# A matmul-bound kernel: the first normalized half cut in two, and the last masks counted longer by the builder

## The chip, the cores and the metric

One core of one Trainium2 chip. The metric is the device time of one execution in microseconds, lower is better; a figure quoted for a kernel is the median of its runs.

The engines go by short names: PE is the matmul engine and PEld its weight loads, DVE the vector engine, ACT the scalar engine, POOL GpSimd. A load "lands" when its data has arrived. Times inside a profile are microseconds from the start of its span.

## The reference

The whole is `x + A(xn) + B(xn)` with `xn = layernorm(x)`, for x of 2048 x 1024 in bf16.

```python
h = _layernorm(x)                               # B is given xn: a second layernorm
u = gelu(einsum('bsd,sf->bdf', h, w1) + b1)     # mixes over the 2048 tokens; F = 3584
y = einsum('bdf,fs->bds', u, w2) + b2
# A: 32 heads of 32, four segments of 512 tokens; in each segment
p = softmax(q k^T * scale + mask)               # causal
o = g * (phi(q) M) / (phi(q) z) + (1 - g) * (p v)
M, z = M + phi(k)^T v, z + sum(phi(k))
# and then o @ wo
```

## The kernel before

Every instruction goes out through a builder that keeps its own clock: each operation has an estimated `ns`, and PE's work in the attention part is ordered by when the builder believes operands ready. A wrong estimate makes no wrong result, only another order. PE is to be kept full with "fill": the matmuls of the second MLP product and of the output projection, in two streams, taken whenever no attention matmul is believed ready.

The start. PE is kept busy with warm-ups, matmuls of zeros, until the first data is there. x comes in 16 row chunks of 128; h is its normalized form, and the chunks are the contraction of the first MLP product, so PE can begin with chunk 0 as soon as its h is there. Eight banks collect four column blocks of w1 by two halves of h.

```python
def warm(self):                                  # N_WARM = 14
    with fw.group(reads=[R[0]], writes=[self.R_bank[7]], ns=self.N_WARM * 300):
        for _ in range(self.N_WARM):
            fw.mm(self.bank(7), z[:, 0:P], z, start=True, stop=True)

def norm_and_first_hidden(self):
    self.stats(0); self.scale(0); self.stats(1)
    self.ln_h(0, 0)          # DVE: half of h, 512 columns
    self.ln_h(0, 1)
    self.scale(1); self.ln_h(1, 0); self.ln_h(1, 1)
    self.early_hidden(0)     # PE: 8 matmuls of 512 columns
    # ... statistics of the later chunks: even ones and chunk 1 on ACT, others on DVE
    self.stats(3, 0); self.stats(3, 1, False)
    self.scale(2); self.ln_h(2, 0); self.ln_h(2, 1)
    self.aggregate(3)
    self.early_hidden(1)
    # ... then chunk after chunk
```

The attention part. The logits come in 46 steps of at most seven banks. ACT takes each bank through the exponential into a slot of pT, POOL masks it there, and "weighings" multiply the slots by v. The results of four heads (a unit) are then combined on DVE, transposed by a transfer and multiplied by wo: the last 72 matmuls of the program are such projections. A step is laid out so:

```python
fl.op({"act": (... exp ..., 575, 488)}, [], [R[slot]], box=box[i], give=True)
ns = 225 + 115 * len(masks)
fl.op({"pool": (... affine_select ..., ns, ns + 30)}, [R[slot]], [R[slot]])
```

The softmax here doesn't subtract the row's maximum and nothing guards it: scores larger than these inputs give would overflow.

## Time and profile before

| | kernel before |
|---|---|
| time, first three runs | 690.88 us (690.82 to 691.54) |
| span of the profile | 689.3 us |
| PE busy | 685.0 us, 99% |
| DVE, ACT, POOL busy | 34%, 45%, 22% |
| first matmul of chunk 0 / first weight load of chunk 3 | 6.64 / 12.44 us |
| last step's logits / last 72 projections start | 666.07 / 672.90 us |

The page's first part says who is full; here only PE. The chain of waits then says which of the few idle times of PE matter: it goes back from the last instruction to whatever released each step. Everything that lies ahead of 12.44 us on that chain is ACT, DVE, POOL and a landing. The lines are in the prediction.

### The profile page before, as it was taken

The numbers are of one execution on the slowest core, as the hardware profiler recorded it, in microseconds if no ns is written. First come the engines' busy times: TensorE is split into PE (matmuls) and PEld (weight loads), VectorE is DVE, ScalarE is ACT, GpSimd is POOL, SyncE is SP. The second block draws the span as 40 slices with busy tenths as digits, with TensorE's granted clock in tenths as the row PEclk, the third lists the DMA queues.
The fourth block names the chain that finished last, engine by engine and source line by source line (L and its number), as shares of the span: only waits on it lengthen the run. The fifth ranks groups of instructions, "written<-read, shape, count | busy, mean of one in ns | idle before, by whom it ended". The sixth has DMA issues, their size and how long they took to land.

```text
span 689.3 us, 12154 instructions
## 1 busy us (share of the span) xinstructions
PE 685.0 (99%) x4855; PEld 327.3 (47%) x4855; DVE 234.8 (34%) x505; ACT 309.6 (45%) x611; POOL 153.9 (22%) x379
## 2 busy tenths in 40 slices
PE   9999999999999999999999999999999999999998
PEld 3444444444444454444454444544544444544554
DVE  6631100000001242434462461743636333451524
ACT  7331111111134475755645472745756453544540
POOL 4820000000001232323312131313333131312330
DMA  9367666325027657657547566474564546445334
GB/s 310 119 178 182 160 156 202 100 61 144 1 93 169 147 133 151 143 121 183 131 95 166 123 134 143 100 170 99 131 145 108 124 115 156 106 104 139 79 86 137
DMA packets 275714, 92.06 MB, mean 134 GB/s; under 512 B 234186, under 2 KB 272074, under 8 KB 275658
## 3 DMA queue, kind: packets, MB, share of 16 engines
q1 hardware_dynamic: 275658, 91.28, 53.5%
q8 instruction: 39, 0.64, 0.4%
q14 instruction: 17, 0.14, 0.1%
HBM read 74.47 MB, written 5.24 MB: 116 GB/s over the span
## 4 chain that ended last, share of the span: by engine, by line
PE 97%; ACT 1%; DMA 1%; POOL 0%; DVE 0%; SPq 0%; issue 0%; POOLq 0%; DVEq 0%
PE ps_all L217 97%; DMA xin<-in_A_x_dram 1%; ACT xn_tmp L850 0%; POOL pT L1158 0%; DVE h L891 0%; SPq L247 0%; ACT xn_tmp L852 0%; ACT pT L1150 0%; POOL ln_r L883 0%; POOLq L581 0%; DVE fin L1356 0%; POOL ln_t L881 0%; DVE ln_mv L866 0%; DVEq L65 0%
## 5 line engine op out<-in xcount | busy, mean ns | idle before, releaser
L1158 POOL TENSOR_SCALAR_AFFINE_SELECT pT<-pT 128x256 bf16<-128x256 bf16 (+1 forms) x320 | 127.6, 408 | 504.2 <-ACT pT L1150 494.7
L1150 ACT ACTIVATE pT<-ps_all 128x512 bf16<-128x512 f32 x320 | 161.9, 618 | 76.8 <-PE ps_all L217 76.8
L217 PE MATMUL ps_all<-h,w1all 128*128 128x512 bf16 x896 | 193.9, 379 | 0.3 <-DVE h L891 0.2
L217 PEld LDWEIGHTS ps_all<-h,w1all 128*128 128x128 bf16 x896 | 87.5, 98 | 106.5 <-issue 0.9
L217 PE MATMUL ps_all<-gT,w2n 128*128 128x512 bf16 x560 | 124.1, 379 | 0.0
L1005 ACT ACTIVATE gT<-ps_all,bc 128x512 bf16<-128x512 f32 x56 | 37.8, 690 | 140.6 <-PE ps_all L217 140.6
L217 PE MATMUL ps_all<-gT,w2l 128*128 128x512 bf16 x325 | 86.0, 380 | 0.0
L217 PEld LDWEIGHTS ps_all<-gT,w2n 128*128 128x128 bf16 x560 | 54.4, 98 | 64.0 <-DMA w2n<-in_B_w_dram 0.2
L1220 ACT ACTIVATE ost<-ps_all 128x264 bf16<-128x264 f32 (+1 forms) x97 | 34.0, 379 | 75.3 <-PE ps_all L217 74.0
L1479 DVE SCALAR_TENSOR_TENSOR stg<-ps_all,bc,stg 128x512 bf16<-128x512 f32 x32 | 23.9, 746 | 124.9 <-PE ps_all L217 124.9
L217 PE MATMUL ps_all<-xnT,wk 128*128 128x512 bf16 x256 | 60.5, 379 | 0.0
L217 PE MATMUL ps_all<-xnT,wq 128*128 128x512 bf16 x256 | 60.4, 379 | 0.0
L217 PE MATMUL ps_all<-wv_sb,xnT 128*128 128x512 bf16 x256 | 60.2, 379 | 0.0
L217 PEld LDWEIGHTS ps_all<-vA,pT 128*128 128x128 bf16 x1280 | 41.2, 96 | 5.5 <-POOL pT L1158 1.0
L217 PEld LDWEIGHTS ps_all<-gT,w2l 128*128 128x128 bf16 x325 | 27.6, 97 | 33.7 <-issue 10.1
L217 PE MATMUL ps_all<-vA,pT 128*128 128x33 bf16 x1280 | 42.8, 177 | 0.3 <-POOL pT L1158 0.3
L943 DVE TENSOR_SCALAR gcol<-gcol 128x32 f32<-128x32 f32 x1 | 0.2, 182 | 118.6 <-ACT gcol L941 118.6
L217 PEld LDWEIGHTS ps_all<-xnT,wk 128*128 128x128 bf16 x256 | 25.1, 98 | 30.2
L217 PEld LDWEIGHTS ps_all<-wv_sb,xnT 128*128 128x128 bf16 x256 | 24.9, 98 | 30.5 <-ACT pT L1150 4.0
L1031 ACT ACTIVATE kT<-ps_all 128x512 bf16<-128x512 f32 x32 | 19.1, 597 | 43.2 <-PE ps_all L217 43.2
L217 PEld LDWEIGHTS ps_all<-xnT,wq 128*128 128x128 bf16 x256 | 23.4, 97 | 29.5 <-issue 6.4
L217 PE MATMUL ps_all<-wo_sb,oT 128*128 128x512 bf16 x128 | 31.2, 379 | 0.0
(74 smaller groups left out, 482.9 us busy)
## 6 DMA issues: line engine op xcount, KB each, us to landing
w2n<-in_B_w_dram SPq DMA_DIRECT2D x100, 160.0 KB, 2.7
w1all<-in_B_w_dram SPq DMA_DIRECT2D x12, 1024.0 KB, 5.2
w2l<-in_B_w_dram SPq DMA_DIRECT2D x73, 128.0 KB, 2.4
wq<-in_A_wq_dram SPq DMA_DIRECT2D x32, 256.0 KB, 2.9
wk<-in_A_wk_dram SPq DMA_DIRECT2D x32, 256.0 KB, 3.2
stg<-in_A_x_dram SPq DMA_DIRECT2D x32, 128.0 KB, 2.6
out_dram<-stg SPq DMA_DIRECT2D x32, 128.0 KB, 2.1
xin<-in_A_x_dram SPq DMA_DIRECT2D x5, 512.0 KB, 6.5
```

Source lines behind the costliest of these rows:

```text
L217: ins = self.nc.tensor.matmul(out, *args, **kwargs)
L943: fw.op("dve", lambda e: e.tensor_scalar(self.gcol[:], self.gcol[:], 1.0, None, op0=ALU.add), reads=[self.R_gcol], writes=[self.R_gcol])
L1005: fw.op("act", lambda e: e.activation(self.gT[:, fc, half * 512:(half + 1) * 512], self.bank(b), ACT.Gelu_apprx_tanh, bias=self.b1c[:, fc: ...
L1031: self.flow.op({"act": (lambda e, b: e.activation(dst, view(self.bank(b)), ACT.Copy), 585, 540), "dve": (lambda e, b: e.tensor_copy(dst, v ...
L1150: fl.op({"act": (lambda e, b, slot=slot: e.activation(pT[:, slot, :], self.bank(b), ACT.Exp, scale=SCALE), 575, 488)}, [], [R[slot]], box= ...
L1158: fl.op({"pool": (lambda e, ap=ap, pat=pat: e.affine_select(ap, ap, pattern=pat, compare_op=ALU.is_ge, fill=0.0, base=0, channel_multiplie ...
L1220: "act": (lambda e, b: e.activation(dst, self.ps[:, b, 0:n * VW], ACT.Copy), 175 + n * 27, 140 + n * 27)},
L1479: engs={"dve": (lambda e, b: e.scalar_tensor_tensor(dst, k.bank(b), k.b2c[:, c:c + 1], dst, op0=ALU.add, op1=ALU.add), 750, 785)},
```

## The change

Two things. The first quarter of h of chunk 0 is made apart, so that PE may begin on it sooner. Its bank then has two matmuls for its two column halves, and a start flag on both would not do (the prediction says why), so the last four warm-up matmuls write zeros with the start flag into banks 0, 2, 4 and 6, and the eight quarter matmuls only accumulate. Second, the builder counts the masks of the last two steps 200 ns longer.

```diff
 def warm(self):
-    with fw.group(..., writes=[self.R_bank[7]], ...):
-        for _ in range(self.N_WARM):
-            fw.mm(self.bank(7), z[:, 0:P], z, start=True, stop=True)
+    with fw.group(..., writes=[self.R_bank[b] for b in (0, 2, 4, 6, 7)], ...):
+        for i in range(self.N_WARM):
+            b = 2 * (i - self.N_WARM + 4) if i >= self.N_WARM - 4 else 7
+            fw.mm(self.bank(b), z[:, 0:P], z, start=True, stop=(b == 7))
 # norm_and_first_hidden
-    self.ln_h(0, 0)
+    self.ln_h(0, 0, True)     # two operations of 256 columns, the second waits for the first
 # early_hidden
+    if c == 0:
+        for q in range(2):
+            for fc in range(self.N_EARLY):
+                with fw.group(reads=[self.R_w1f[0], self.R_h[0][0] if q else self.R_h0], ...):
+                    fw.mm(self.ps[:, 2 * fc, 256 * q:256 * q + 256], ...,
+                          self.h[:, 0, 256 * q:256 * q + 256], start=False, stop=False)
 # step
-    ns = 225 + 115 * len(masks)
+    ns = (225 if n < self.n_steps - 2 else 425) + 115 * len(masks)
```

More of the change, by code (lines that the diff above doesn't have):

```diff
@@ L676, in alloc @@
         self.R_xnt = [Res(f"xnt{i}") for i in range(4)]
+        self.R_h0 = Res("h0q")
         self.R_h = [[Res(f"h{c}_{hf}") for hf in range(2)] for c in range(N_TCH)]
@@ L801, in warm @@
         fw.op("dve", lambda e: e.memset(z, 0.0), writes=[R[0]])
-        with fw.group(reads=[R[0]], writes=[self.R_bank[7]], ns=self.N_WARM * 300):
-            for _ in range(self.N_WARM):
-                fw.mm(self.bank(7), z[:, 0:P], z, start=True, stop=True)
+        with fw.group(reads=[R[0]], writes=[self.R_bank[b] for b in (0, 2, 4, 6, 7)], ns=self.N_WARM * 300):
+            for i in range(self.N_WARM):
+                b = 2 * (i - self.N_WARM + 4) if i >= self.N_WARM - 4 else 7
+                fw.mm(self.bank(b), z[:, 0:P], z, start=True, stop=(b == 7))
     def norm_and_first_hidden(self):
@@ L884, in scale, with ln_h @@
               reads=[self.R_rs[c], self.R_mhalf], writes=[self.R_rs[c]], ns=600)
-    def ln_h(self, c, half=None):
+    def ln_h(self, c, half=None, quarter=False):
         fw = self.fw
+        if quarter:
+            fw.op("dve", lambda e: e.tensor_scalar(self.h[:, c, 0:256], self.xin[:, c, 0:256], self.ln_mv[:, c, 0:1],
+                                                   self.ln_r2[:, c:c + 1], op0=ALU.subtract, op1=ALU.mult),
+                  reads=[self.R_xin[c], self.R_mean[c], self.R_rs[c]], writes=[self.R_h0], ns=158)
+            fw.op("dve", lambda e: e.tensor_scalar(self.h[:, c, 256:512], self.xin[:, c, 256:512], self.ln_mv[:, c, 0:1],
+                                                   self.ln_r2[:, c:c + 1], op0=ALU.subtract, op1=ALU.mult),
+                  reads=[self.R_xin[c], self.R_mean[c], self.R_rs[c], self.R_h0], writes=[self.R_h[c][0]], ns=158)
+            return
         a, z = (0, D_MODEL) if half is None else (512 * half, 512 * half + 512)
@@ L898, in early_hidden @@
         last = c == N_TCH - 1
+        if c == 0:
+            for q in range(2):
+                for fc in range(self.N_EARLY):
+                    with fw.group(reads=[self.R_w1f[0], self.R_h[0][0] if q else self.R_h0],
+                                  writes=[self.R_bank[2 * fc]]):
+                        fw.mm(self.ps[:, 2 * fc, 256 * q:256 * q + 256], self.w1first[:, 0, fc * P:(fc + 1) * P],
+                              self.h[:, 0, 256 * q:256 * q + 256], start=False, stop=False)
         order = [(fc, half) for half in range(2) for fc in range(self.N_EARLY)] if c < 3 else \
@@ L901, in early_hidden @@
         for fc, half in order:
+            if c == 0 and half == 0:
+                continue
             b = 2 * fc + half
@@ L1284, in attention_and_out @@
         steps = self.logit_steps()
+        self.n_steps = len(steps)
         first, last = {}, {}
```

## The prediction

> **What bounds the kernel now.** I read the page first, then the waits of the matmul engine, the chain of waits in order of time, and the timeline of the two stretches that the diff touches: the first 13 us and the last 25 us. The page says that there is hardly anything to win:
>
> ```profile
> span 689.3 us, 12154 instructions
> PE 685.0 (99%) x4855; PEld 327.3 (47%) x4855; DVE 234.8 (34%) x505; ACT 309.6 (45%) x611; POOL 153.9 (22%) x379
> ```
>
> PE is busy 99% of the span at a granted clock of 1.000. The waits of PE list three idle times in the whole run:
>
> ```profile
> PE ps_all L217 <- DVE gT L801: 1.3, 1, 1.3
> PE ps_all L217 <- POOL pT L1158: 0.3, 1, 0.3
> PE ps_all L217 <- DVE h L891: 0.2, 1, 0.2
> ```
>
> The 1.3 us is the start of the program, before the warm-up operand is zeroed; the change leaves it alone. The chain of waits says which of the others count:
>
> ```profile
> 6.50 1.16 ACT xn_tmp L850 x2
> ...
> 9.89 0.73 DVE h L891 x2
> ...
> 11.84 0.56 DVE h L891
> 12.40 0.05 issue
> 12.44 654.06 PE ps_all L217 x4562
> ...
> 667.68 1.54 POOL pT L1158 x2
> 669.22 0.44 POOLq L581
> 669.66 0.05 issue
> 669.71 17.21 PE ps_all L217 x125
> ```
>
> Up to 12.44 us the chain is not the matmuls at all: it is the landing of the third row chunk of x (6.47), its statistics on ACT, h of chunk 2 (9.89), and then statistics and h of chunk 3 (11.84). From 12.44 PE runs through to 669.71, where it waited for a mask on POOL, and then through to the end. So only two things can move the end: when h of chunk 3 is there, and the hole before 669.71.
>
> The timeline around the first real matmul, in narrow windows (PE's shown durations hold some 0.17 us of drain; the spacing of the starts is the stream):
>
> ```profile
> 6.43 0.38 PE L217 MATMUL ps_all<-gT 128*128 128x512 bf16 x1
> 6.64 0.38 PE L217 MATMUL ps_all<-h,w1all 128*128 128x512 bf16 x1
> 6.01 0.41 DVE L891 TENSOR_SCALAR h<-xin,ln_mv,ln_r 128x512 bf16<-128x512 bf16 x1 [0.68 <-POOL ln_r L883]
> 10.45 2.82 PE L217 MATMUL ps_all<-h,w1all 128*128 128x512 bf16 x11 [0.19 <-DVE h L891]
> ```
>
> The last warm-up starts at 6.43 and the first real matmul at 6.64, one warm spacing later. The first half of h was finished at 6.42. PE did not wait for h there.
>
> The hole near the end, with the last masks:
>
> ```profile
> 669.00 0.38 PE L217 MATMUL ps_all<-gT,w2l 128*128 128x512 bf16 x1
> 669.71 0.27 PE L217 MATMUL ps_all<-vA,pT 128*128 128x33 bf16 x4 [0.33 <-POOL pT L1158]
> 667.68 0.73 POOL L1158 TENSOR_SCALAR_AFFINE_SELECT pT<-pT 128x256 bf16<-128x256 bf16 x1
> 668.37 0.85 POOL L1158 TENSOR_SCALAR_AFFINE_SELECT pT<-pT 128x256 bf16<-128x256 bf16 x1
> 669.18 0.47 POOL L1158 TENSOR_SCALAR_AFFINE_SELECT pT<-pT 128x128 bf16<-128x128 bf16 x1
> 669.61 0.40 POOL L1158 TENSOR_SCALAR_AFFINE_SELECT pT<-pT 128x256 bf16<-128x256 bf16 x1
> ```
>
> The last unit's first weighing (four matmuls of 33 columns) needs the fourth of the last step's five masks, the 128x128 one that ends at 669.65. The hole is listed as 0.33, but a 512-column matmul streams for 0.216 us (28 of them from 657.17 to 663.22), so PE was really empty from 669.22 to 669.71, 0.49 us.
>
> **What the Trainium skill says.** "TensorE: Matmul & The Clock Gate", Part 1: 426.7 ns from start to start at 512 columns cold, 215.7 warm. The trace agrees: warm-up weights load every 0.43 us up to 5.92, and real matmuls follow at 0.216. "VectorE: DVE Perf Modes", The TRN2 errata: each SBUF-source operation pays a fixed cost, so halving it does not halve the time. The trace agrees: h takes 0.414 us at 512 columns and 0.547 at 1024. "PSUM — Partial Sum Buffer", The four PSUM rules: a first matmul with the start flag clears the accumulate bits of the whole bank. That is why the four banks are opened by zero matmuls: two quarter matmuls that both start would undo each other. No run here shows it. "SBUF — State Buffer", Who interferes with whom: a VectorE operation with two SBUF inputs contends with GpSimd's reads. The trace fits: the 0.73 and 0.85 us masks lie beside the two products of the combining step on DVE (0.83 and 0.89 us from 667.31), while the median mask is 0.408.
>
> **Part 1, the first quarter of h.** The warm-up keeps its 14 matmuls; four only go to other banks, so it still ends at 6.64. From the two h sizes, a column costs (0.547 - 0.414) / 512 = 0.26 ns, so 256 columns take an estimated 0.414 - 0.067 = 0.35 us. The first quarter is there at about 6.36 instead of 6.42: 0.06 us earlier, in front of a PE that is busy until 6.64. Gain at that place: none. Cost: the second quarter waits for the first by semaphore, 6.01 + 0.35 + about 0.05 = 6.41, ending at 6.76; the other half of h then ends near 7.15 instead of 6.75. PE wants the second quarters at 6.64 + 4 x 0.109 = 7.08 and the other half at about 7.52, so neither is waited for. Eight matmuls of 256 columns stream for 8 x 0.109 = 0.87 us in place of 4 x 0.216 = 0.86. The weight load (0.098) fits under each.
>
> What becomes of any tenth won or lost here: PE finishes chunk 1 at about 10.26 and waits 0.19 for h of chunk 2, then finishes chunk 2 near 12.15 and waits 0.29 for h of chunk 3. Both come from ACT and DVE. An earlier start only lengthens those waits. DVE is free at about 7.15 and idles until 7.65 in any case. So part 1 is worth 0.0, with perhaps 0.1 lost if POOL's small operations for chunk 1 (6.07 to 7.51) are slowed by the longer DVE run.
>
> **Part 2, masks counted longer.** This changes no instruction, only the clock by which the builder orders PE's work, and only for the last two of 46 steps (the steps' own rule gives 46; the last has five masks, the one before seven). It counted 225 + 115 or 230 ns, 340 or 455, where the last five really took 0.41, 0.73, 0.85, 0.47 and 0.40. So it believed the weighing ready when it was not. With 200 ns more per mask, POOL is the slower one in its book (455 + 200 + 30 = 685 a piece against 488 for the exponentials). The fourth mask ends later there by about 200 + 3 x (685 - 488) = 0.8 us. That makes room for 0.8 / 0.216, three or four more fill matmuls ahead of the weighing. They exist: after the 12 of the long stream there is one more, and eight of the output projection, which PE did at 669.88, 670.10 and 671.40. Four take PE from 669.22 to 670.08, past the mask's end at 669.65. The hole of 0.49 is filled. The book may be a matmul short or long, so I count 0.45.
>
> For the step before, two weighings of unit 30 come later in the book, but they ran at 664.94 after a whole group of 36 fill matmuls, while their masks were done by 658.3. Nothing to gain, little to lose.
>
> Does the end follow? After the last weighing the final 72 projection matmuls run from 672.90. They need the last transposed piece only at the 36th, about 680.5; its transpose is issued at 675.31 and lands some 2.3 us later. There are 2 us to spare, and the weighings do not end later than before, since fill goes in front of them but out of their middle.
>
> Sum: 0.0 + (-0.45) = -0.45 us on 690.88, so 690.4.
>
> **Rivals.** (a) Both parts are worth nothing: the order shifts, but another wait opens, such as the weighing of the second query block on the fifth mask (ends 670.01). For it: masks vary with what DVE does beside them. Against: four fills alone already run past 670.01. Time 690.9. (b) The first part does work, because in a timed run the clock comes up earlier and PE then waits for h: at most 0.06 to 0.1 at that place, and the waits for chunks 2 and 3 still take it. Time as predicted. (c) Reordering in the last two steps moves a whole group of fill ahead of the logits, and the last combining lands late: more than 2 us of slack would have to go. Time 691 to 693. (d) The longer DVE run delays h of chunk 3, which is on the chain: up to 0.3 us back, 690.7.
>
> **Range and chances.** The three runs before span 0.72 us (690.82 to 691.54), larger than the effect; the best case is about 690.3, and rivals (a) and (d) reach 690.9. I take 689.9 to 691.1. Two per cent is 13.8 us; PE is 99% busy and idles 0.5 us in the parts touched, so faster by that is out of reach, and slower needs a broken schedule.
>
> **What would show it.** Right: the first real matmul still at about 6.6, chunk 3 still starting near 12.44 with longer waits before it, no wait of PE on a mask, 15 or 16 fill matmuls in place of 12 before the last weighings, and the end about 0.45 earlier. Wrong: chunk 3 starting earlier than 12.4 (part 1 is worth something), a remaining mask wait, or a DMA wait in the last 72 matmuls.

## The result, and the profile after

The changed kernel took 690.72 us in the median of six runs (690.39 to 691.06), the kernel before 691.04 in the six beside them (690.82 to 691.54). The ratio is 0.9994, 95% interval 0.9981 to 1.0007. Ratios here are the mean time of one kernel's runs over that of the other's of the same rounds, so not quite the ratio of the medians. The timing alone calls it the same; what happened has to be read from the traces.

The page of the changed kernel, its first two lines, and the whole list of PE's waits:

```profile
span 689.0 us, 12163 instructions
PE 685.1 (99%) x4859; PEld 327.4 (48%) x4859; DVE 235.1 (34%) x506; ACT 309.4 (45%) x611; POOL 153.8 (22%) x379
```

```profile
PE ps_all L217 <- DVE gT L802: 1.3, 1, 1.3
```

The wait on the mask is gone, and so is the listed wait on h. Four more matmuls and one more DVE operation are the quarter. The chain of waits (start, length, what):

```profile
9.71 0.74 DVE h L901 x2
...
11.66 0.56 DVE h L901
12.22 0.05 issue
12.26 622.21 PE ps_all L217 x4280
...
634.53 4.51 DMA w2n<-in_B_w_dram
639.04 0.05 issue
639.08 47.54 PE ps_all L217 x400
```

The head of the chain is as before, 0.18 us sooner. A load of w2 (into the buffer w2n) that took 4.51 us to land (the median is 2.6) now stops PE at 639, for 0.25 us. The end has no stop any more. The start in the timeline:

```profile
6.00 0.35 DVE L891 TENSOR_SCALAR h<-xin,ln_mv,ln_r 128x256 bf16<-128x256 bf16 x1 [0.68 <-POOL ln_r L885]
6.55 7.62 PE L217 MATMUL ps_all<-h,w1all 128*128 128x256 bf16 x36
```

The first quarter was ready at 6.35 and PE came to it at 6.55, from the warm-ups. And the end, with two of the masks:

```profile
666.83 2.98 PE L217 MATMUL ps_all<-gT,w2l 128*128 128x512 bf16 x13
669.64 0.81 PE L217 MATMUL ps_all<-wo_sb,oT 128*128 128x512 bf16 x3
670.29 0.26 PE L217 MATMUL ps_all<-vA,pT 128*128 128x33 bf16 x4
668.58 0.85 POOL L1177 TENSOR_SCALAR_AFFINE_SELECT pT<-pT 128x256 bf16<-128x256 bf16 x1
669.38 0.47 POOL L1177 TENSOR_SCALAR_AFFINE_SELECT pT<-pT 128x128 bf16<-128x128 bf16 x1
```

Sixteen fill matmuls stand ahead of the weighing in place of twelve, the mask takes as long as before and ends at 669.85, and PE, which comes to it at 670.29, does not wait.

Cut at two landmarks, the difference of 0.29 us (the last DVE addition starts at 686.65 instead of 686.94) falls into three pieces:

| stretch | before | after | difference |
|---|---|---|---|
| to the first weight load of chunk 3 | 12.44 | 12.26 | -0.18 |
| from there to the last step's logits | 653.63 | 654.02 | +0.39 |
| from there to the last addition | 20.87 | 20.37 | -0.50 |

The built order of PE's instructions differs in only two places, the quarter and the last step. So the middle row has no cause in PE's order (it is nearly all in PE's stops for loads of w2, 0.12 us at 392 and 0.25 at 639), and the open question is the first row: does the quarter give 0.18?

### The profile page after: what moved, and what is told of

The parts are those of the page before. It is cut to its first block, busy times and chain, and to the rows that moved or that the text cites. A ratio compares the mean times of both kernels' runs of the same rounds, so it can differ in the third digit from the quotient of the medians.

```text
span 689.0 us, 12163 instructions
## 1 busy us (share of the span) xinstructions
PE 685.1 (99%) x4859; PEld 327.4 (48%) x4859; DVE 235.1 (34%) x506; ACT 309.4 (45%) x611; POOL 153.8 (22%) x379
## 4 chain that ended last, share of the span: by engine, by line
PE 97%; DMA 1%; ACT 1%; DVE 0%; POOL 0%; issue 0%; SPq 0%; DVEq 0%
PE ps_all L217 97%; DMA w2n<-in_B_w_dram 1%; ACT xn_tmp L852 0%; DMA xin<-in_A_x_dram 0%; ACT xn_tmp L854 0%; DVE h L901 0%; POOL ln_r L885 0%; SPq L247 0%; DVE fin L1376 0%; POOL ln_t L883 0%; DVE ln_mv L868 0%; DVEq L65 0%
## 5 line engine op out<-in xcount | busy, mean ns | idle before, releaser
L217 PE MATMUL ps_all<-h,w1all 128*128 128x512 bf16 (+1 forms) x900 | 193.9, 378 | 0.2
```

Source lines behind the costliest of these rows:

```text
L217: ins = self.nc.tensor.matmul(out, *args, **kwargs)
```

## The experiments

Twelve kernels ran. The first four tell the parts apart and measure how much a profile moves by itself.

**Masks only** (the kernel before plus the last hunk of the diff).

> The kernel before with the masks of the last two steps counted longer, nothing else. My theory: this is the whole of the change's worth. PE should show no wait on a mask, and from the start of the last step's logit matmuls to the first of the 72 last projections some 0.49 us less than before (6.83 us there, 6.33 here); the whole run 0.3 to 0.6 us faster than before, ratio about 0.9993. Rival (the quarter of h carries part of it): the time lies between before and after, less than 0.3 us gained.

690.76 us (690.55 to 691.45, five runs), ratio 0.9993 (0.9980 to 1.0005). No mask wait; from the last logits (666.23) to the last projections (672.57) 6.34 us. This has the whole gain at the end. And without the quarter its chunk 3 started at 12.27. Its list of PE's waits has no mask, but a load of w2:

```profile
PE ps_all L217 <- DVE gT L801: 1.3, 1, 1.3
PE ps_all L217 <- DMA w2n<-in_B_w_dram: 0.2, 1, 0.2
```

**Quarter only** (the changed kernel with the old `ns`).

> The changed kernel with the masks counted as before: only the first quarter of h is left. My theory: worth 0.0; the mask wait of 0.33 us before the last unit's weighing is back, the ratio is 1.000 within 0.001, and matmuls of chunk 3 start when its h is there (about 12.3 to 12.4), not sooner for the earlier first matmul. Rival: the earlier start is passed on and chunk 3 starts 0.1 to 0.2 us sooner than in a run of the kernel before, as the changed kernel's trace seems to show (12.26 against 12.44).

690.98 us (690.82 to 691.24), ratio 0.9995 (0.9982 to 1.0007). PE's waits:

```profile
PE ps_all L217 <- DVE gT L802: 1.2, 1, 1.2
PE ps_all L217 <- DVE h L891: 0.8, 1, 0.8
PE ps_all L217 <- POOL pT L1177: 0.3, 1, 0.3
```

The mask wait is back. There is also something that the prediction had as a rival only: in this run the clock came up early, the warm-ups were over sooner, and PE did wait for the first quarter. Even so, chunk 3 (second line: PE's weight loads) was held by its own h, which ended at 12.29:

```profile
11.74 0.55 DVE L901 TENSOR_SCALAR h<-xin,ln_mv,ln_r 128x1024 bf16<-128x1024 bf16 x1 [0.54 <-POOL ln_r L885]
12.34 0.33 PEld L217 LDWEIGHTS ps_all<-h,w1all 128*128 128x128 bf16 x3 [0.60 <-DVE h L901]
```

**Both kernels once more**, unchanged.

> The kernel before, unchanged, once more: how far two profiles of one kernel differ by themselves. My theory: the start of chunk 3 moves by 0.1 to 0.2 us with the landing of the x chunks, and single waits for a w2n load of 0.3 us come and go, so this profile may show 12.26 or 12.44; the mask wait of 0.33 us is there again; ratio 1.000. Rival: the start at 12.44 is this kernel's own and comes again within 0.03.

> The changed kernel, once more. My theory: no mask wait, the stretch from the last step's logits to the 72 last projections again 6.33 us, the start of chunk 3 anywhere between 12.2 and 12.5, ratio about 0.9993. Rival: chunk 3 starts at 12.26 again within 0.03, and the load wait of 0.26 us at 639 is there again.

The kernel before: 691.03 us (690.82 to 691.76), ratio to its own other runs 0.9998 (0.9984 to 1.0011), chunk 3 at 12.17 and the mask wait at 0.32. The changed kernel: 690.92 us (690.51 to 691.55), ratio 0.9995 (0.9983 to 1.0008), chunk 3 at 12.38, no mask wait, 6.34 us from the logits to the last projections, and no load wait at 639. So the start of chunk 3 wanders by 0.27 us in the kernel before alone (12.17 to 12.44), the order of the two kernels is turned round, and the 0.18 and the load wait at 639 are the run's, not the change's. The traces also show what moves the start. ACT begins the statistics of chunk 2 when the third row chunk of x has landed, or when it is done with chunk 1. That was at 6.50 and 6.25 in the kernel before and at 6.32 and 6.44 in the changed one, and chunk 3 loaded 5.94, 5.91, 5.94 and 5.94 us after it.

**The quarter where PE does wait: 10 warm-ups in place of 14**, in either kernel.

```diff
-    N_WARM = 14
+    N_WARM = 10
```

> The kernel before with 10 warm-up matmuls in place of 14, so that PE is idle when the first h comes and the quarter could show. My theory: the first real matmul starts about 0.15 us after the end of the first half of h (0.41 us after that operation's start), whichever that is; chunk 3 still starts 0.05 us after the end of its own h, near 12.2 to 12.4, if the clock is up by 8 us; time unchanged within 0.1%. Rival: fewer warm-ups raise the clock later and chunk 3 starts after 12.6.

> The changed kernel with 10 warm-ups. My theory: the first real matmul now comes 0.06 us sooner after the start of the first h operation than in the kernel before with 10 warm-ups (0.35 in place of 0.41, plus the same delay), and chunk 3 starts no sooner for it: 0.05 us after its own h. Rival (the quarter is worth what it saves when PE waits for it): chunk 3 starts sooner against its own h's chain, and the run gains another 0.1 us.

In both, PE waited for h (0.9 and 1.4 us). The first real weight load came 0.53 us after the start of the first h operation without the quarter (6.62 after 6.09) and 0.46 with it (6.53 after 6.07). So the quarter saves 0.07 us at its place. Chunk 3 in the run with it: h ended at 12.23, weight load at 12.28. Nothing passed on. The run without it went otherwise than expected: its clock came up only after 10 us, chunk 0 and the first matmul of chunk 1 ran at half speed, its profile is 690.4 us long, and it took 691.59 us (691.20 to 692.14; ratio 1.0003, 0.9987 to 1.0018). The one with the quarter took 690.81 (690.52 to 691.18; 0.9991, 0.9976 to 1.0006). With clocks that differ so, these two times are not to be compared with each other.

**A later start: 18 warm-ups**, in the changed kernel.

> The changed kernel with 18 warm-ups, four of 0.216 to 0.427 us more, so the first real matmul comes 0.9 us later, near 7.4. My theory: the slack ahead of chunk 3 is about 0.5 us (0.19 + 0.29 in the kernel before), so PE no longer waits for h of chunks 2 and 3 and chunk 3 starts 0.2 to 0.5 us later than 12.35, at 12.6 to 12.9. Rival (no slack, the start of PE is what counts): 0.9 us later, at 13.2.

Missed, on the safe side: 690.60 us (690.46 to 691.27), ratio 0.9990 (0.9972 to 1.0008). The clock was up at 5.0 us in this run, so four more warm-ups moved the first matmul only to 6.93. That is 0.38 later than in the changed kernel's profile, and chunk 3 still loaded at 12.24, 0.05 after its h. It shows slack of that much, and leaves open where it ends (a run below tells).

**Why the masks were late: products with one input** (the kernel before; the result is wrong on purpose, relative error 196).

```diff
 for k, to, R_to in ((0, os, R_os), (1, self.prod, self.R_prod)):
+    if u == 30:
+        dve(<reciprocal of v into pk>, R_ost + [R_rec], [R_to], 700)
+        continue
     dve(<v times rk, both in SBUF>, R_ost + [R_rec], [R_to], 700)
```

> The kernel before, with the two products of unit 30's combining step on DVE replaced by reciprocals of one input each (a wrong result on purpose, the schedule untouched). My theory: those two-input products slow the masks beside them; with one input the masks of the last step take about 0.41 us each (they were 0.73 and 0.85), the fourth ends before 669.2, and the mask wait before the last weighing is gone or under 0.1 us without the longer count. Rival (the masks are slow by themselves, or by DMA): they stay above 0.65 and the wait of 0.3 is there.

Two masks and the weighing behind them in this run:

```profile
668.14 0.41 POOL L1158 TENSOR_SCALAR_AFFINE_SELECT pT<-pT 128x256 bf16<-128x256 bf16 x1
668.63 0.29 POOL L1158 TENSOR_SCALAR_AFFINE_SELECT pT<-pT 128x128 bf16<-128x128 bf16 x1
669.18 0.26 PE L217 MATMUL ps_all<-vA,pT 128*128 128x33 bf16 x4
```

All four two-block masks took 0.41, the single one 0.29, though DVE was busy beside them for longer than before. The wait was gone with the old count. So the products are what stretched 0.41 to 0.73 and 0.85. (The single mask lay beside the sum that follows them, also of two inputs.)

This run leaves one rival: a reciprocal also takes four times as long over the same columns, so its slower pace, and not its single input, may be what spared the masks. The rest of the trace of the kernel before speaks against that. There 43 two-block masks lay beside casts out of PSUM, and three beside a cast and an addition of one tensor in SBUF and one in PSUM. Beside these operations at their usual pace the masks took 0.40 to 0.41 as well. Nine masks beside a product and the sum behind it took 0.85.

The run as a whole was slower, 694.64 us (693.45 to 695.66; ratio 1.0046, 1.0026 to 1.0065; profile at a clock of 0.998): each reciprocal took 3.3 us, the last unit's combining fell behind, and within the last 72 projections PE waited 2.7 us for its transpose. Lateness is only part of it: the transpose was issued 2.8 us later than in the kernel before (678.08 for 675.31), and it also took 4.7 us to land in place of 2.4. About one microsecond after the wait, PE's matmuls started 0.43 us apart in place of 0.216, from 683.9 to 687.3, which cost another 1.7 us. So this run shows what a late last piece looks like, but not how late the combining alone may be.

**How much to count: 100 ns, and 600 ns**, in the changed kernel.

```diff
-    ns = (225 if n < self.n_steps - 2 else 425) + 115 * len(masks)
+    ns = (225 if n < self.n_steps - 2 else 325) + 115 * len(masks)     # the other kernel: 825
```

> The changed kernel with 100 ns more per mask instead of 200. The order it builds has two fill matmuls (one of w2, one projection) more than before ahead of the last unit's first weighing, in place of four. My theory: the hole of 0.49 us shrinks by 2 x 0.216 to about 0.06, so from the last logits to the first weighing 3.6 to 3.7 us with PE barely waiting, and the stretch to the 72 last projections 6.35 to 6.45 us against 6.83 and 6.33. Rival (the whole re-timing counts, not the number of matmuls in the hole): it stays at 6.8.

> The changed kernel with 600 ns more per mask: all nine fill matmuls go ahead of the weighings. My theory: no wait on a mask, the stretch to the last projections the same 6.33 us; the last unit's combining comes about 0.6 us later than in the changed kernel and still well ahead of its use, so the time is as the changed kernel's. Rival (the later combining is felt): PE waits on the last transpose within the 72 projections.

With 100 ns: 690.88 us (690.60 to 691.13), ratio 0.9994 (0.9981 to 1.0006). Two more fill matmuls are enough but for a sliver: the last starts at 669.41, its 0.216 us end at 669.63, the weighing starts at 669.67, and from the logits to the last projections it takes 6.39 us. With 600 ns all nine go ahead: 690.52 us (690.49 to 691.01), ratio 0.9991 (0.9978 to 1.0003), 6.33 us, and PE waits for no transpose. Counting the last step alone, and not the one before it, builds the same instructions in the same order on every engine as the change does; that was compared and not run.

**Moving what does set the start**: the aggregation of chunk 3's statistics ahead of h of chunk 2, with and without the quarter.

```diff
     self.scale(2)
+    self.aggregate(3)
     self.ln_h(2, 0)
     self.ln_h(2, 1)
-    self.aggregate(3)
```

> The changed kernel with one DVE operation moved: the aggregation of chunk 3's statistics ahead of h of chunk 2 instead of behind it. My theory says h of chunk 3 is what starts the matmul run, so this should show there: h of chunk 3 ends 0.3 to 0.5 us sooner after h of chunk 2 begins, chunk 3's matmuls follow chunk 2's without a wait, about 0.15 to 0.25 us sooner than before against the start of h of chunk 2, which itself may start up to 0.1 later. Time 0.1 to 0.2 us below the changed kernel, inside the noise. Rival: h of chunk 2 is delayed by as much as is won.

> The same move without the quarter of h (the masks counted longer). My theory: the quarter is worth nothing here either, since PE still waits for h of chunk 2; chunk 3 starts at the same distance from the start of h of chunk 2 as in the run with the quarter, within 0.05 us. Rival: without the wait on chunk 3 the earlier first matmul is passed on and the quarter is worth 0.05 to 0.1 us.

Without the quarter, h of chunks 2 and 3 and PE's weight loads from chunk 2 on:

```profile
9.91 0.72 DVE L891 TENSOR_SCALAR h<-xin,ln_mv,ln_r 128x512 bf16<-128x512 bf16 x2
11.16 0.55 DVE L891 TENSOR_SCALAR h<-xin,ln_mv,ln_r 128x1024 bf16<-128x1024 bf16 x1
10.42 3.58 PEld L217 LDWEIGHTS ps_all<-h,w1all 128*128 128x128 bf16 x18 [0.70 <-issue]
```

The wait between chunks 2 and 3 is gone; chunk 3's first matmul starts at 12.18, 2.27 us after h of chunk 2 begins, against 2.55 in the kernel before (12.44 after 9.89) and in the changed one (12.26 after 9.71): 0.28 sooner. But the expectation's rival is more than half of that: h of chunk 2 itself now waits for the aggregation. It begins 0.32 us after POOL's scale for chunk 2 (9.59), against 0.14 in both other kernels (after 9.75 and 9.57). From POOL's end, chunk 3 comes after 2.58 us in place of 2.70 and 2.69. So h of chunk 3 was the bound, and one DVE operation of 0.21 us in another place gains some 0.11 us there, where the quarter gains nothing. With the quarter, the same move met a late clock: the first full-speed matmul came at 7.17, h of chunk 3 was done at 11.62, and PE ran through without a wait at its own pace, so this profile tells nothing of the quarter either way, and its comparison stays open. It does show where the slack ends: PE alone took 5.19 us from its first matmul to chunk 3 (7.17 to 12.36), while the changed kernel took 5.71 (6.55 to 12.26), so it had some 0.5 us to spare. Neither run kept its gain up to the last logits (666.14 without the quarter, 666.36 with it): PE stopped for loads of w2, for 0.33 us at 392 and for 0.36 at 639. In time: 690.60 us with the quarter (690.34 to 690.87; ratio 0.9989, 0.9976 to 1.0003), 690.75 without (690.07 to 690.96; 0.9991, 0.9978 to 1.0003). They are the lowest ratios here together with the 600 ns count, but within the noise of the changed kernel; a version that beats it is not shown.

**All profiles side by side.** "To chunk 3" is its first weight load (in brackets the end of its own h), the last column runs from the last step's logits to the start of the last addition.

| profile | quarter | count | to chunk 3 | last logits | last stretch |
|---|---|---|---|---|---|
| before | no | old | 12.44 (12.39) | 666.07 | 20.87 |
| before again | no | old | 12.17 (12.12) | 666.02 | 20.85 |
| quarter only | yes | old | 12.34 (12.29) | 665.98 | 20.86 |
| masks only | no | +200 | 12.27 (12.21) | 666.23 | 20.37 |
| after | yes | +200 | 12.26 (12.21) | 666.28 | 20.37 |
| after again | yes | +200 | 12.38 (12.33) | 666.01 | 20.37 |
| 100 ns | yes | +100 | 12.41 (12.36) | 666.05 | 20.42 |
| 600 ns | yes | +600 | 12.57 (12.52) | 666.24 | 20.36 |

The last column moves with the count alone and repeats to 0.02 us. Chunk 3 always starts 0.05 us after its own h, with or without the quarter.

The table has one more thing to say, of the middle. From chunk 3 to the last logits it takes 653.6 to 653.7 us in five of the profiles and more in three, and what is more are stops of PE for loads of w2: 0.21 in the repeat of the kernel before (at 371), 0.32 with the masks only (at 371), 0.37 in the changed kernel (at 392 and 639). These three are the ones whose chunk 3 started before 12.3. An early start was thus taken back on the way, in part or altogether: the repeat of the kernel before started 0.27 us sooner than its first profile and reached the last logits 0.05 sooner. Why the loads are late in these runs was not examined.

In time, the changed kernel, its repeat and the five other kernels with a longer count and 14 warm-ups have 36 runs with a mean of 690.77 us; the runs without it (the kernel before, the repeat of it, and the quarter alone, 34 runs) have 691.24. That is 0.46 less, pooled over calls and variants and so no strict comparison; it agrees with the 0.49 of the trace, but not every pairing does. In the first call of the study alone, masks only and the repeat of the changed kernel have a mean of 690.94, quarter only and the repeat of the kernel before 691.09, which is 0.14 less. The timings leave the size of the gain open.

## Why the prediction was right

The time was predicted at 690.4 in a range of 689.9 to 691.1, and the mechanism holds.

- **The hole of 0.49 us before the last weighing is filled.** Shown: the last stretch is 0.50 shorter after the change and 0.50 shorter with the mask count alone. The prediction counted 0.45 for fear of a matmul short or long; four went in, as worked out, and 100 ns would already have left only 0.05 us.
- **The masks are slow because of DVE's two-input products beside them.** The prediction only said that the trace fits. Shown by the one-input run, and by the masks beside casts and PSUM additions in the kernel before.
- **The quarter is worth 0.0.** Shown at both levels: it saves 0.07 us where PE waits for it (0.06 was worked out), and chunk 3 does not move with it. The prediction said that PE does not wait for the first h at all, since the warm-ups end later; that is true only of runs in which the clock comes up late. In the quarter-only profile PE waited 0.77 us. The second line of the argument, the waits for chunks 2 and 3, carried it. The room there is larger than the 0.19 and 0.29 that were read: by the starts, with 0.216 for a matmul, PE stood empty for 0.35 us before chunk 2 (9.88 to 10.45) and 0.28 before chunk 3 (11.95 to 12.44).
- **The longer DVE run costs nothing.** With the quarter, h of chunk 3 ended between 12.21 and 12.52 in the table, without it between 12.12 and 12.39. Counted from the start of ACT's statistics of chunk 2, where the landing no longer matters, chunk 3 loads after 5.91 to 5.94 us in the three profiles of the table without the quarter and in the five with it. So it costs nothing there beyond 0.03 us, and it gains no more.
- **The last combining has 2 us to spare.** Shown in part: with all nine fill matmuls ahead of the weighings no wait appeared, and the transposed piece landed at 678.21, 1.9 us before the 36th projection (680.12). The one wait that was seen, in the one-input run, needed a transpose 2.8 us late and a landing of 4.7 us as well.
- **What was wrong** is the test that the prediction set itself: chunk 3 starting before 12.4 was to mean that part 1 is worth something. It started at 12.26, and part 1 is worth nothing. The kernel before gives 12.17 by itself. A landmark from one profile was taken for a constant, when it hangs on a landing: the third row chunk of x landed at 6.47 in the kernel before, at 5.57 in its repeat and at 6.30 in the changed kernel, and the statistics and h of chunk 3 follow behind.
- **The size in time.** 0.32 us between the medians and 0.49 by the trace. In the profiled pair, the middle of the changed kernel's run is 0.39 us longer, by stops for loads of w2 such as masks only and the repeat of the kernel before have too, and its head 0.18 shorter, by the landing. With the 0.50 at the end that leaves the 0.29 between the two profiles; the load stops are not shown to come from the change.

## What to carry to other kernels

Where a builder orders the work by its own clock, look for the places where the profile shows a wait that the builder did not expect: there an operation is dearer than its estimate, here because of what ran beside it. It is mended by the estimate alone, no instruction has to change. And before a first operation is cut finer, look at what the engine waits for next: an earlier start in front of a later wait is worth nothing, and a landmark that hangs on a clock or a landing has to be seen in several profiles before it is believed.

## What the Trainium skill lacked or had wrong

- "TensorE: Matmul & The Clock Gate", Part 1, gives the transition as about 4 us into the activity, 500 ns either way. Here, with the warm-ups always starting at 1.25 us, full speed began between about 4.1 us (quarter only) and about 7.1 us (aggregation moved, with the quarter), some 3 to 6 us in. In one of the two runs with 10 warm-ups and a pause behind them it began only after 10.0 us. The same page's remark that the number of cold matmuls differs from run to run fits: 7 to 14 here, in the runs with 14 warm-ups.
- "SBUF — State Buffer", Who interferes with whom, says that a DVE operation with two SBUF inputs contends with a GpSimd instruction that reads SBUF and that one with at most one, outside the modes that use both ports, does not. That fits here, but the page gives no size for a mask: 0.41 us alone became 0.73 and 0.85 beside the products, and 0.41 again beside one-input operations.
- "VectorE: DVE Perf Modes", The TRN2 errata, puts the fixed cost at 58 cycles in its table and at about 150 by its own measurement (some 60 and 156 ns at the page's 0.96 GHz). For the operation that makes h the runs give 0.35, 0.41 and 0.55 us for 256, 512 and 1024 columns, and a line through the last two leaves some 280 ns.
- No page gives the time of a reciprocal on DVE: 0.35 us for 128x32 and 3.35 us for 128x512 here, some 6 ns a column.
